# A rearranged prologue, transfers kept in written order, and loads spread over more slots in a Nystrom attention and feed-forward kernel

## The chip, the cores and the metric

The kernel runs on one core of one Trainium2 chip. The metric is the device time of one execution in microseconds (us). Three timed runs of the kernel before took 836.07, 836.29 and 840.3 us; their median is 836.29 us. One more execution was profiled, and it took 832.87 us.

## The reference

The attention runs over 4 batches, 8 heads, 576 positions and 64 features per head. It uses 32 landmarks, each the mean of 18 positions, and six Newton-Schulz steps for an inverse. Two feed-forward layers follow, both without biases:

```
q_lm, k_lm = means of 18 positions of q and k
A  = softmax(q @ k_lm^T / 8);  Bm = softmax(q_lm @ k_lm^T / 8);  C = softmax(q_lm @ k^T / 8)
Z  = Bm^T / (norm_1(Bm) * norm_inf(Bm) + 1e-6)
six times:  Z = 2 Z - Z @ Bm @ Z
x  = A @ Z @ C @ v                        # then heads side by side: 2304 tokens x 512
y  = ((x @ w_a) * (x @ w_b)) @ w_out      # 512 -> 1536 -> 512
h  = y @ w_in2
out = (h * tanh(softplus(h))) @ w_out2    # 512 -> 2048 -> 512
```

The three weights of the first layer and the two of the second lie in memory as 64-bit floats.

## The kernel before

**The work.** The whole program is one function, `nystrom_moe_kernel`. The attention of a batch is a list of steps: `kl`, `ql` (landmark sums), `sB` and `BB` (the landmark softmax and its norms), six `NS` (Newton-Schulz), `sC0`, `sC1` (scores of the landmarks against all keys), `ET0`, `ET1` (transposes), `U` (product with v), `M` (product of inverse and U, 128 x 128), `A0`, `A0n`, `A1`, `A1n` (scores of all queries, in two halves, and their normalisation). `fold` multiplies `M` into a block of the first layer's weights (tile `wab`) and gives `bm`, so that the first layer is `at` times `bm`. A slot (`ab`, then `emit_o1`) is 128 columns of the hidden layer for 288 tokens: 6 matmuls into bank `ps_ab` for each of w_a and w_b, their product `tg` on VectorE, its split in a high and a low part `g`, and 12 matmuls `ps_o<-g,wo` that add to the first output `x2acc`. There are 96 slots, and `CELLS` orders them by eights. Phase two takes 768 tokens at a time: seven products of 384 columns (`ps_ab<-xc,wc`) stand in for eight blocks, and `ps_o`, `ps_at` and `ps_bm` collect the output.

**Conversion.** Each 64-bit weight block of 128 x 512 (a unit) is loaded into a `stg` tile, turned to float32 by one ScalarE and four VectorE instructions (`to_f32`), and used or stored. The first layer has 36 units (24 for `wab`, 12 for `wo1`). The 32 of the second layer go through a buffer `f24` to memory (`wi2d`, `wo2d`) and are loaded again later.

**Order.** Up to slot 11 the order of TensorE, VectorE and ScalarE is written out by hand in the table `ORDER_1`, one word per piece: an attention step of batch 0, with `+` of batch 1, `cN` a piece of conversion unit N, `sN` of slot N, `oN` of an output, `f`/`F` a fold, and a bare number that many filling matmuls of the identity. `Written` holds instructions to program order while it is on. After slot 11 it is off: the loop over slots emits the work, and a scheduler that sees the whole program orders it. All transfers go out on one queue, SP, which issues them one by one; a transfer whose semaphore has not come holds those behind it.

**The places that the change touches.** In the prologue the landmark sums of batch 1 come from token tiles `tok` (`load_tokens`, L125; `lm_sum`, L162 on). They are 20 matmuls each for k and q: 128 tokens-by-feature columns are the fixed side, `blk` with 7 columns the moving one. `u0.prefetch` (L399) loads the units, eight of them early. In the slots, `load_wab` (L474) and `load_wo1` (L501) fetch weights again, `u2.step` runs the second layer's units from slot 45 to 84, `to_dram` (L604) stores each, and the store of `x2acc` (L586) follows its twelfth sum at once. `x_early` (from slot 82) prepares the first inputs of phase two, and its `weight_sums` puts two subtractions per weight on GpSimd (L430).

Of the kernel before, what the change touches and what calls it, by code (L numbers as in the profile page):

```python
# [31 lines left out]
def nystrom_moe_kernel(ctx: ExitStack, tc: tile.TileContext, q, k, v, w_a, w_b, w_out1, w_in2, w_out2, q1, k1, out):  # L32
# [35 lines left out]
    main = main_ctx.enter_context(tc.tile_pool(name="main", bufs=1, side="left"))  # L68
    p1_ctx = ExitStack()
# [16 lines left out]
    ist = const.tile([128, 1, 32], F32, name="ist")  # L86
    ist2 = ist.to_broadcast([128, 2, 32])
    blk = const.tile([128, 7], F32, name="blk")
# [3 lines left out]
    def consts():  # L92
        make_identity(nc, ident)
        gp.memset(bdm, 0.0)
        gp.memset(ones, 1.0)
        for h in range(4):
            gp.memset(bdm[32 * h:32 * h + 32, 32 * h:32 * h + 32], 1.0)
        ve.tensor_reduce(out=blk, in_=ident[:, 0:126].rearrange("p (l k) -> p l k", k=BLK), axis=AX, op=ALU.add)
        ve.tensor_reduce(out=ist[:, 0], in_=ident.rearrange("p (h l) -> p l h", h=4), axis=AX, op=ALU.add)
# [49 lines left out]
    def attention(ap, b, kt, qt, vt0=None, tokens=None):  # L149
# [226 lines left out]
    N_UNITS, N_SLOTS = 20, 12  # L376
    ORDER_1 = """
        kl kl ql ql c0 sB sC0 sB c0 sB sC1 4 c1 sC0 sB c2 sC1 BB 2 sC1 c3 BB sC1 sC1 c2 NS 2 c1 c3 NS ET0 NS
        c0 NS 2 c1 ET0 ET1 c3 c1 NS A0 ET1 NS c1 NS 1 A0 U NS A0 NS A0 c3 NS +kl U NS NS A0 c3 NS c0 +kl NS A0
        c0 NS +ql c2 c2 NS A0n c4 +ql NS +ql c5 c2 A0n M c6 +kl c5 M c5 A0n c5 f0 c7 A0n A1 c7 f0 c7 +kl A1 c8  # L380
        f0 +ql +kl A1 | s0 +ql c7 A1 +sC0 c5 +sC1 +sC0 s0 s0 A1 +sC1 s1 +sC1 A1 s0 c7 c6 s1 s1 A1n s0 s0 A1n
        c6 +sC1 s1 c6 +sC1 +sB c6 A1n +ET0 +sB s1 A1n +sB s1 +ET0 +sB s2 +ET1 c4 s2 c4 +BB c4 +ET1 s2 c4 +BB
        +U s2 c8 s2 +NS +U s2 s3 +NS +NS c8 +NS c8 s3 s3 +NS +NS c9 c8 +NS s3 f1 c8 c9 +NS +NS s3 c9 +NS c8 s3
        f1 c9 +NS c10 +NS f1 +NS +NS +NS s4 c10 c9 +NS s4 c10 s4 c9 +NS s5 s4 c10 s4 +M s5 s4 c10 s5 +M c9 c10
        s6 s5 c11 c10 +A0 s6 c11 s5 s6 c11 s5 c11 c12 s7 s6 c11 F0 s7 s6 +A0 c11 s6 s7 +A0 F0 +A1 c11 +A0 s7
        o0 F0 +A0 c12 o1 c12 +A0 c12 c12 o0 c13 F1 +A0n o1 s7 o2 c13 F1 s7 +A0n F1 +A0n o3 o2 +A0n c13 s8 c13
        c14 c13 o3 o4 s8 c14 c14 c14 c15 s8 +A1 o4 s9 c15 s8 o5 s9 +A1 s8 s8 c14 +A1 s9 c15 c15 c16 s10 s9 +A1
        c16 o6 c16 c16 s10 +A1 c15 s10 c16 o5 s11 +A1n o6 c17 o7 s9 s10 s11 +A1n s9 s10 c17 +A1n s11 s10 c17
        o7 c17 +A1n c18 s11 c18 s11 c18 s11 c17 c19 c18 c19 c19 c18 c19 c19
    """  # L390

    def stage(src, shape, early):

        tag, bufs = ("w", 8) if early else ("stg", 3)
        t = (main if early else base).tile([128, 512, 2], U32, tag=tag, bufs=bufs, name="stg")
# [36 lines left out]
    class Units:  # L432


        def __init__(self, units, early=0):
            self.units, self.st, self.n, self.ahead, self.early = units, [], 0, 2, early

        def prefetch(self, ahead=0):
            while len(self.st) < min(len(self.units), self.n + max(self.ahead, ahead)):
                src, shape, _ = self.units[len(self.st)]  # L440
                self.st.append(stage(src, shape, len(self.st) < self.early))
# [13 lines left out]
    def wab_units(g):  # L455
        def conv(i, jj, st):
# [3 lines left out]
            yield from to_f32(t[:, 2 * jj:2 * jj + 2, i], st, True)  # L460
            converted[g] = converted.get(g, 0) + 1
# [4 lines left out]
        for jj in range(2):  # L466
            for i, w in enumerate((w_a, w_b)):
                src = w.bitcast(U32)[256 * jj:256 * jj + 256, 512 * g:512 * g + 512].rearrange("(j p) f -> p j f", p=128)
                out.append((src, 2, lambda st, i=i, jj=jj: conv(i, jj, st)))
        return out  # L470

    def load_wab(g):
        t = wab[g] = main.tile([128, 4, 2, 256], F32, tag="wab", bufs=3, name="wab")
        nc.sync.dma_start(out=t.rearrange("p j i f -> p (j i f)"), in_=wabd[g])  # L474

    def split_unit(dst_hi, dst_lo, st):
# [9 lines left out]
        (gp if u0.n == 36 else ve).tensor_tensor(dst_lo, f3, dst_hi.bitcast(F32), op=ALU.subtract)  # L486

    wo1 = {}
    wo1d = [dram.tile([128, 2, DM], F32, name=f"wo1d{c}") for c in range(12)]

    def wo1_unit(c):
        def conv(st):
            wo1[c] = main.tile([128, 2, DM], F32R, tag="w", bufs=8, name="wo1")
# [5 lines left out]
    def load_wo1(c):  # L499
        wo1[c] = main.tile([128, 2, DM], F32R, tag="w", bufs=8, name="wo1")  # L500
        nc.sync.dma_start(out=wo1[c].bitcast(F32), in_=wo1d[c])  # L501
# [36 lines left out]
    def ab(b, g, hf, ch, gpool=None):  # L538
# [9 lines left out]
        if gpool is None:  # L548
            t = p1.tile([128, 2, 288], F32R, tag="g", bufs=9, name="g1")
# [10 lines left out]
    o1p, o1n = {}, {}  # L560

    def emit_o1(b, gp_, hf, d, part, now=True):
# [13 lines left out]
        def evict():  # L576
# [8 lines left out]
            if o1n[b, hf] == 12:  # L585
                nc.sync.dma_start(out=x2d[b][:, :, 288 * hf:288 * hf + 288], in_=x2acc[b, hf])  # L586
# [9 lines left out]
    f_pool = []  # L596

    def to_dram(dst, st):
        if f_pool:
# [472 lines left out]
```

## Time and profile before

| | |
|---|---|
| median of 3 timed runs | 836.29 us |
| profiled execution | 832.87 us |
| its span, first to last instruction | 830.8 us |
| mean granted TensorE clock | 0.982 |
| TensorE (PE) busy | 794.9 us, 96% |
| VectorE (DVE) busy | 545.8 us, 66% |
| ScalarE (ACT) busy | 359.3 us, 43% |
| GpSimd (POOL) busy | 144.1 us, 17% |
| moved by DMA | 183.45 MB, mean 221 GB/s |

PE, DVE, ACT and POOL are the four engines, PEld is TensorE loading its fixed side, and SP is the queue of transfers. A busy PE need not be at full speed, for a granted clock of 0.5 doubles the time of the same matmuls. A line number such as L56 belongs to a helper for most instructions, so groups are told apart by the tiles they write and read.

### The profile page before, as it was taken

To read this page: it belongs to the slowest core of one execution; us is meant where nothing else is said; L and a number is where in the kernel's file an instruction comes from. 1 tells how busy PE (TensorE), PEld (TensorE's weight loads), DVE (VectorE), ACT (ScalarE), POOL (GpSimd) and SP (SyncE) were. 2 spreads that over 40 slices of the span, in tenths; PEclk is the share of its full clock that TensorE was granted. 3 is DMA by queue.
4 is the path that set the end of the run, shared out by engine and by line. 5 is a ranking of instruction groups with operands and counts; after the bars stand their busy time and mean duration, and the time that the engine had idled before them with its cause. 6 is when DMAs were issued, how large, how long until landed. Compare 5 with 4: busy or idle time off the path is not lost.

```text
span 830.8 us, 14869 instructions
## 1 busy us (share of the span) xinstructions
PE 794.9 (96%) x5882; PEld 699.9 (84%) x5882; DVE 545.8 (66%) x1024; ACT 359.3 (43%) x826; POOL 144.1 (17%) x140
## 2 busy tenths in 40 slices
PE   5978899999999999899999999999999999999998
PEld 4766788987887797899899888998999999899997
DVE  7588897796585787988944767867433447433433
ACT  3555765434333544444533553454332335332332
POOL 0012022122240232222332354330000000000000
PEclk9679999999999999999999999999999999999999
DMA  9957567559326937978417887788654554654502
GB/s 333 341 207 242 191 231 242 187 166 332 128 87 217 361 99 258 330 247 308 130 58 269 295 298 258 291 302 332 239 213 182 190 188 179 251 212 171 190 1 76
DMA packets 48733, 183.45 MB, mean 221 GB/s; under 512 B 4260, under 2 KB 12452, under 8 KB 39320
## 3 DMA queue, kind: packets, MB, share of 16 engines
q1 hardware_dynamic: 48664, 182.51, 61.8%
q8 instruction: 46, 0.75, 0.4%
q14 instruction: 23, 0.19, 0.1%
HBM read 129.02 MB, written 53.48 MB: 220 GB/s over the span
## 4 chain that ended last, share of the span: by engine, by line
PE 76%; DVE 9%; DMA 7%; ACT 4%; issue 2%; POOL 1%; SPq 0%; DVEq 0%; ACTq 0%
PE ps_ab L56 33%; PE ps_o L56 23%; PE ps_bm L56 10%; PE ps_at L56 9%; DVE f L56 2%; DMA tok<-in_q_dram 2%; DMA s_out<-wo2d 2%; DMA wi2d<-f 2%; ACT sa L56 1%; DMA stg<-in_moe_w_a_dram 1%; DVE tg L56 1%; DMA stg<-in_moe_w_in_dram 1%; DVE f L413 1%; POOL wo L430 1%; DVE stA L56 1%
## 5 line engine op out<-in xcount | busy, mean ns | idle before, releaser
L56 PE MATMUL ps_ab<-xc,wc 128*128 128x384 f32 x1008 | 198.2, 336 | 1.8 <-DVE xc L56 1.1
L56 PE MATMUL ps_ab<-at,bm 128*128 128x288 f32 x1152 | 187.9, 304 | 3.8 <-DVE tg L56 2.8
L56 PEld LDWEIGHTS ps_ab<-xc,wc 128*128 128x128 f32 x1008 | 178.7, 188 | 13.1 <-DVE xc L56 1.4
L56 PE MATMUL ps_o<-g,wo 128*128 128x288 f32 x1152 | 180.0, 298 | 7.1 <-DVE x2acc L56 4.9
L56 PEld LDWEIGHTS ps_ab<-at,bm 128*128 128x128 f32 x1152 | 162.8, 191 | 25.6 <-issue 8.1
L56 PEld LDWEIGHTS ps_o<-g,wo 128*128 128x128 f32 x1152 | 161.0, 188 | 19.9 <-DVE x2acc L56 6.7
L555 POOL TENSOR_TENSOR g<-tg,g 128x288 fp32r<-128x288 f32 x96 | 84.8, 884 | 319.5 <-ACT g L56 319.5
L56 ACT ACTIVATE m<-c 128x384 f32<-128x384 f32 x95 | 49.7, 524 | 175.7 <-DVE c L56 175.3
L56 PE MATMUL ps_bm<-wo,g 128*128 128x512 f32 x288 | 93.4, 391 | 0.3 <-ACT g L56 0.3
L56 DVE TENSOR_TENSOR g<-m,g 128x384 fp32r<-128x384 f32 x96 | 66.0, 690 | 29.5 <-ACT g L56 29.4
L56 PE MATMUL ps_at<-wo,g 128*128 128x512 f32 x288 | 82.0, 391 | 0.0
L56 ACT ACTIVATE g<-tg 128x288 fp32r<-128x288 f32 x96 | 42.6, 444 | 86.3 <-DVE tg L56 85.9
L56 PE MATMUL ps_o<-wo,g 128*128 128x512 f32 x288 | 78.7, 391 | 0.9 <-DVE g L56 0.9
L56 DVE SCALAR_TENSOR_TENSOR f<-stg,f 128x512 uint32<-128x512 uint32 x88 | 68.8, 787 | 1.2
L56 DVE TENSOR_TENSOR tg<-ps_ab,ta 128x288 f32<-128x288 f32 x96 | 43.2, 451 | 31.3 <-PE ps_ab L56 17.1
L56 PEld LDWEIGHTS ps_at<-wo,g 128*128 128x128 f32 x288 | 53.9, 188 | 9.7
L56 PEld LDWEIGHTS ps_o<-wo,g 128*128 128x128 f32 x288 | 53.6, 188 | 10.1 <-DVE g L56 1.3
L56 PEld LDWEIGHTS ps_bm<-wo,g 128*128 128x128 f32 x288 | 53.3, 188 | 6.8 <-ACT g L56 0.6
L56 ACT ACTIVATE ta<-ps_ab 128x288 f32<-128x288 f32 x96 | 38.8, 405 | 42.8 <-PE ps_ab L56 42.2
L56 ACT ACTIVATE g<-m 128x384 fp32r<-128x384 f32 x96 | 50.2, 524 | 2.6
L56 DVE TENSOR_TENSOR c<-ps_ab,m 128x384 f32<-128x384 f32 x23 | 12.8, 558 | 48.2 <-PE ps_ab L56 48.2
L56 DVE TENSOR_TENSOR u2s<-ps_ab,m 128x384 f32<-128x384 f32 x24 | 13.3, 555 | 42.7 <-PE ps_ab L56 42.7
(150 smaller groups left out, 819.5 us busy)
## 6 DMA issues: line engine op xcount, KB each, us to landing
wc<-wcd SPq DMA_DIRECT2D x16, 1792.0 KB, 8.2
wo<-wod SPq DMA_DIRECT2D x16, 1024.0 KB, 5.5
stg<-in_moe_w_out_dram SPq DMA_DIRECT2D x28, 512.0 KB, 4.7
wcd<-wc SPq DMA_DIRECT2D x8, 1792.0 KB, 5.8
wab<-wabd SPq DMA_DIRECT2D x10, 1024.0 KB, 8.4
stg<-in_moe_w_in_dram SPq DMA_DIRECT2D x16, 512.0 KB, 5.8
wod<-wo SPq DMA_DIRECT2D x8, 1024.0 KB, 7.4
stg<-in_moe_w_a_dram SPq DMA_DIRECT2D x12, 512.0 KB, 3.6
```

Of the source, the lines that this page charges most:

```text
L56: i = f(*a, **kw)
L413: i = ve.engine.tensor_scalar(dst, dst, F32_TINY, F32_HUGE, op0=ALU.max, op1=ALU.min)
L430: lo_eng.tensor_tensor(dst_lo, src, dst_hi.bitcast(F32), op=ALU.subtract)
L555: gp.tensor_tensor(t[:, 1], tg, t[:, 0].bitcast(F32), op=ALU.subtract)
```

## The change

1. **Token sums.** The tokens are now the moving side: five matmuls of 32 x 512 per sum, four of them in different column groups, then a copy `lsum` on ScalarE and four matmuls of 128 x 32 with `sel` that gather and transpose.
2. **Prologue.** The first eight conversion units are joined in four of twice the width (`wab_units(..., double)`), so units 0 to 19 are now 0 to 15. The four later loads of them stand ahead of the token loads. `ORDER_1` is new: `sC0` and `sC1` come ahead of `sB`, and other fills stand between the `NS` steps.
3. **Written order.** `late` chains the transfers from slot 36 on, each issued after the one written before it.
4. **Stores later.** A store of `x2acc` is written four slots after its last sum, a store of a converted unit after the next unit's conversion.
5. **Loads spread.** Tables give the slot of each load (`WAB_AT`, `WO1_AT`, `X_AT`) and each unit (`U2_AT`, slots 38 to 80); from slot 56 unit loads run four ahead and use two more buffers.
6. **Around phase two.** The low parts in the early `weight_sums` go to VectorE in place of GpSimd; the first weight fetches and the splits for products 5, 4 and 3 are written among the last outputs of phase one, and all seven products of the first block are pinned.

```diff
@@ lm_sum (sums of tokens)
-                for j in range(4):
-                    for i in range(5):
-                        n, r = (4, 72) if i == 4 else (7, 126)
-                        f0 = DM * (i % 2) + 128 * j
-                        pe.matmul(p[:, LM * j + 7 * i:LM * j + 7 * i + n], ts[i // 2][0:r, f0:f0 + 128], blk[0:r, 0:n], start=True, stop=True)
-                    yield
+                for i in (1, 2, 3, 0, 4):
+                    r, g = (72, 0) if i == 4 else (126, i)
+                    pe.matmul(
+                        p[32 * g:32 * g + 32, :], blk[0:r, 0:32] if i == 4 else blk[0:r, 7:39], ts[i // 2][0:r, DM * (i % 2):DM * (i % 2) + DM],
+                        start=(i < 4), stop=(i > 0),
+                    )
+                yield
+                e = pg.tile([128, 2, 288], F32R, tag="g", bufs=4, name="lsum").bitcast(F32).rearrange("p a s -> p (a s)")
+                ac.activation(e[:, 0:DM], p, AF.Copy)
+                yield
+                p = bank("o1")
+                for j in range(4):
+                    pe.matmul(p[:, LM * j:LM * j + LM], e[:, 128 * j:128 * j + 128], sel, start=True, stop=True)
...
-    N_UNITS, N_SLOTS = 20, 12
+    N_UNITS, N_SLOTS = 16, 12
...
+    chain = []
+
+    def late(f):
+
+        def call(*a, **kw):
+            if not chain:
+                return f(*a, **kw)
+            if chain[-1] is None:
+                chain.append(f(*a, **kw).ins)
+                return
+            with tc.issue_after(chain[-1]):
+                chain.append(f(*a, **kw).ins)
...
@@ emit_o1, evict
             if o1n[b, hf] == 12:
-                nc.sync.dma_start(out=x2d[b][:, :, 288 * hf:288 * hf + 288], in_=x2acc[b, hf])
+                i = lambda: late(nc.sync.dma_start)(out=x2d[b][:, :, 288 * hf:288 * hf + 288], in_=x2acc[b, hf])
+                stores.append((at[0] + 4, i))
...
@@ to_dram
-        if f_pool:
-            f = f_pool[0].tile([128, 2 * 2 * TB], F32, tag="xe", bufs=4, name="f24")[:, 0:512]
+        n = u2.n - 1
+        if f_pool and n % 4 > 1:
+            f = f_pool[0].tile([128, 2 * 2 * TB], F32, tag="xf", bufs=2, name="f24")[:, 0:512]
...
-        nc.sync.dma_start(out=dst, in_=f if len(dst.shape) == 2 else f.rearrange("p (j f) -> p j f", j=dst.shape[1]))
+        while unit_stores:
+            unit_stores.pop()()
...
-    def weight_sums(dst, src, t):
+    def weight_sums(dst, src, t, lo=gp, pin=False):
...
@@ before the first table
-    u0.prefetch(4)
-    vt0 = load_v(ap, 0)
+    u0.prefetch(2)
+    vt0 = load_v(ap, 0)
+    u0.prefetch(4)
     tokens = load_tokens()
-    u0.prefetch(8)
...
-    LOAD_W = {5: 0, 6: 1, 7: 0, 8: 1, 9: 2}
-
+    X_AT = {78: -6, 80: -3, 81: -4, 82: 0, 83: 4, 84: -5, 86: 6, 88: 1, 89: 2, 90: 3, 92: 5}
+    U2_AT = [38 + 2 * n for n in range(6)] + [50 + 1.2 * n for n in range(26)]
+    WAB_AT = {37: 0, 38: 1, 42: 2, 49: 3, 52: 0, 56: 1, 62: 2, 66: 3, 72: 4, 75: 5}
+    WO1_AT = {40: 0, 41: 1, 43: 2, 44: 3, 50: 4, 51: 5, 52: 6, 53: 7, 76: 8, 77: 9, 78: 10, 79: 11}
...
-        if ci in LOAD_W and ks in (2, 5):
-            load_wab(2 * LOAD_W[ci] + ks // 4)
-        if ci in (5, 6, 9) and ks >= 4:
-            load_wo1(4 * LOAD_W[ci] + ks - 4)
+        if si in WAB_AT:
+            load_wab(WAB_AT[si])
+        if si in WO1_AT:
+            load_wo1(WO1_AT[si])
```

**TensorE, prologue, batch 0 from the fifth Newton-Schulz step to the first slot.** In these rows `rz` is a Newton-Schulz step, `zd,U` is `M`, `wab,mt` a fold, `qt,kl` is `A1`, and `at,bm` a slot. Before, around `M`:

```order
L56 MATMUL ps_o_490<-blk,tok 128x4
L56 MATMUL ps_o_490<-blk,tok 128x7 x4
L56 MATMUL ps_o_490<-blk,tok 128x4
L56 MATMUL ps_at<-zd,U 64x128 x2
L56 MATMUL ps_o_444<-blk,tok 128x7 x4
L56 MATMUL ps_o_444<-blk,tok 128x4
L56 MATMUL ps_bm<-wab,mt 32x512 x8
L56 MATMUL ps_at<-qt,kl 32x288 x8
L56 MATMUL ps_o_444<-blk,tok 128x7 x4
```

Now:

```order
L56 MATMUL ps_at<-rz 32x64 x8
L56 MATMUL ps_o_472<-ident 128x128 x2
L56 MATMUL ps_at<-rz 32x32 x8
L56 MATMUL ps_o_496<-ident 128x128
L56 MATMUL ps_at<-zd,U 64x128 x2
L56 MATMUL ps_o_510<-tok,blk 32x512 x5
L56 MATMUL ps_at<-qt,kl 32x288 x8
L56 MATMUL ps_bm<-wab,mt 32x512 x8
L56 MATMUL ps_o_551<-tok,blk 32x512 x5
L56 MATMUL ps_o_567<-sel,lsum 128x32 x4
L56 MATMUL ps_ab<-at,bm 128x288 x6
```

All 40 token matmuls stood ahead of the first slot, 25 of them ahead of `M`; now no token matmul stands ahead of `M`, and ten wide ones and four of 128 x 32 stand ahead of the first slot.

**VectorE, prologue, from the start values of Newton-Schulz (`rz<-bc,stB`).** `wab` is conversion. Before:

```order
L56 TENSOR_TENSOR rz<-bc,stB 128x64
L413 TENSOR_SCALAR wab<-wab 128x2x256 x3
L56 TENSOR_TENSOR rz<-ps_at,rz 128x64
L56 TENSOR_SCALAR wab<-wab 128x2x256 x3
L56 SCALAR_TENSOR_TENSOR wab<-stg,wab 128x2x256
L56 TENSOR_TENSOR rz<-ps_at,rz 128x64
```

Now, from a little earlier:

```order
L56 STREAM_TRANSPOSE bc<-bc 128x32 x2
L56 TENSOR_SCALAR wab<-wab 128x1024
L452 TENSOR_SCALAR wab<-wab 128x1024
L56 TENSOR_REDUCE stB<-ps_at 128x2x2
...
L56 TENSOR_TENSOR rz<-bc,stB 128x64
L56 SCALAR_TENSOR_TENSOR wab<-stg_168,wab 128x1024
L56 TENSOR_TENSOR rz<-ps_at,rz 128x64
L56 TENSOR_SCALAR wab<-wab 128x1024
```

Three wide conversion instructions now stand ahead of the start values, where one narrow one stood, and one wide one between one step and the next. At the reduction for batch 1's `sC0` 23 of the 32 narrow instructions of the first eight units were done; now 15 of the 16 wide ones are.

**SP, around the second loads of the first layer's saved weights.** `wabd` holds these weights, `stg` is a 64-bit load, `f` a converted unit. Before:

```order
L474 DMA wab<-wabd_84 128x2048
L604 DMA wi2d_102<-f_3288 128x512
L399 DMA stg<-in_moe_w_out_dram 128x1024
L474 DMA wab<-wabd_85 128x2048
L604 DMA wi2d_102<-f_3355 128x512
L399 DMA stg<-in_moe_w_in_dram 128x2x512
```

Now:

```order
L418 DMA x2d_84<-x2acc 512x1x288
L438 DMA stg<-in_moe_w_in_dram 128x2x512
L438 DMA stg<-in_moe_w_out_dram 128x1024 x2
L418 DMA wo2d_115<-f_3881 128x512
L418 DMA wab<-wabd_88 128x2048
L438 DMA stg<-in_moe_w_in_dram 128x2x512
L418 DMA wo2d_115<-f_3956 128x512
```

Two loads of `wab`, a megabyte each, stood one unit apart; now one stands here, with a store of `x2acc` between, and each store of a unit stands behind the load of a later unit.

## Rows read from the trace of the kernel before

**Rows 1.** Page: granted TensorE clock in 40 slices, in tenths.

```profile
PEclk9679999999999999999999999999999999999999
```

**Rows 2.** Stretches: span, busy time per engine, granted clock, DMA share, GB/s.

```profile
25.30:49.20 23.90, 23.53 (x178) 19.16 (x177) 13.17 (x28) 11.49 (x49) 0.00 (x0) 0.50 0.98 360
49.20:112.00 62.80, 53.41 (x595) 42.95 (x587) 55.47 (x124) 42.82 (x156) 9.74 (x11) 0.95 0.58 202
112.00:190.00 78.00, 77.98 (x602) 67.42 (x602) 66.26 (x127) 36.42 (x79) 18.48 (x20) 1.00 0.61 206
190.00:250.00 60.00, 58.24 (x646) 49.63 (x645) 39.15 (x81) 22.15 (x51) 17.89 (x20) 1.00 0.49 173
250.00:345.00 95.00, 90.89 (x925) 75.55 (x924) 73.76 (x152) 42.96 (x93) 22.74 (x25) 1.00 0.71 255
400.00:443.00 43.00, 39.88 (x293) 38.82 (x292) 28.40 (x51) 20.38 (x40) 18.36 (x17) 1.00 0.33 116
443.00:490.00 47.00, 44.30 (x240) 40.21 (x240) 29.92 (x44) 20.32 (x36) 15.89 (x9) 1.00 0.86 298
490.00:827.00 337.00, 336.69 (x1688) 303.71 (x1686) 174.24 (x292) 125.90 (x232) 26.78 (x12) 1.00 0.56 206
```

**Rows 3.** TensorE in order of time, prologue: start, length, instructions, wait before.

```profile
16.42 0.43 PE L56 MATMUL ps_at<-rz 32*32 32x64 f32 x16 [1.39 <-DVE rz L56]
22.96 0.61 PE L56 MATMUL ps_o<-blk,tok 126*128 126x7 f32 x4
...
29.55 1.44 PE L56 MATMUL ps_o<-blk,tok 126*128 126x7 f32 x6 [0.37 <-DMA tok<-in_q_dram]
30.92 0.44 PE L56 MATMUL ps_at<-rz 32*32 32x32 f32 x16
31.29 4.43 PE L56 MATMUL ps_o<-blk,tok 126*128 126x7 f32 x20
35.65 0.70 PE L56 MATMUL ps_at<-zd,U 128*64 128x128 f32 x4
...
38.50 1.96 PE L56 MATMUL ps_bm<-wab,mt 64*32 64x512 f32 x16
...
45.63 1.79 PE L56 MATMUL ps_ab<-at,bm 128*128 128x288 f32 x6
47.35 1.21 PE L56 MATMUL ps_at<-kt,ql 64*32 64x288 f32 x16
...
66.07 0.43 PE L56 MATMUL ps_at<-rz 32*32 32x64 f32 x16
...
67.42 0.43 PE L56 MATMUL ps_at<-rz 32*32 32x64 f32 x16
67.78 1.09 PE L56 MATMUL ps_bm<-wab,mt 64*32 64x512 f32 x16
```

**Rows 4.** VectorE in order of time, prologue.

```profile
26.56 0.42 DVE L56 TENSOR_SCALAR wab<-wab 128x512 uint32<-128x512 uint32 x1
44.27 1.28 DVE L56 SCALAR_TENSOR_TENSOR wab<-stg,wab 128x512 uint32<-128x512 uint32 x2
48.67 0.76 DVE L56 TENSOR_REDUCE stC<-ps_at 128x2 f32<-128x576 f32 x1 [3.12 <-PE ps_at L56]
...
111.92 0.45 DVE L56 TENSOR_TENSOR tg<-ps_ab,ta 128x288 f32<-128x288 f32 x1
```

**Rows 5.** Waits of TensorE: total us, times, longest.

```profile
PE ps_o L56 <- DVE x2acc L56: 4.9, 4, 1.9
```

**Rows 6.** SP in order of time: the load of batch 1's keys.

```profile
31.58 0.33 SPq L111 DMA_DIRECT2D kt<-in_k_dram  x1
```

**Rows 7.** DMA issues: KB each, median us from issue to landing.

```profile
kt<-in_k_dram SPq DMA_DIRECT2D x3, 1152.0 KB, 13.3
```

**Rows 8.** Chain of work that ended last, 240 to 345 us: start, length, what.

```profile
267.95 9.66 DMA wi2d<-f
...
325.85 5.77 DMA stg<-in_moe_w_in_dram
```

More of the change, by code (lines that the diff above doesn't have):

```diff
@@ new lines, in stage @@
+    def stage(src, shape, early, spare=None):
+        if early:
+            t = main.tile([128, 2 * DM, 2], U32, tag="w", bufs=4, name="stg2")
+            v = t.rearrange("p (j i f) w -> p j i (f w)", j=2, i=2)
+            for i, a in enumerate(src):
+                late(nc.sync.dma_start)(out=v[:, :, i], in_=a)
+            return t
+        if spare:
+            t = spare.tile([128, 2 * 7 * 2 * 128], F32, tag="we", bufs=2, name="stg")
+            t = t[:, 0:1024].bitcast(U32).rearrange("p (n w) -> p n w", w=2)
+        else:
+            t = base.tile([128, 512, 2], U32, tag="stg", bufs=3, name="stg")
@@ L459, in conv @@
             t = wab[g]
-            yield from to_f32(t[:, 2 * jj:2 * jj + 2, i], st, True)
-            converted[g] = converted.get(g, 0) + 1
+            half = t[:, 2 * jj:2 * jj + 2]
+            yield from to_f32(half.rearrange("p j i f -> p (j i f)") if double else half[:, :, i], st, True)
+            converted[g] = converted.get(g, 0) + 1 + double
             if converted[g] == 4:
@@ L499, in load_wo1 @@
     def load_wo1(c):
-        wo1[c] = main.tile([128, 2, DM], F32R, tag="w", bufs=8, name="wo1")
-        nc.sync.dma_start(out=wo1[c].bitcast(F32), in_=wo1d[c])
+        wo1_tile(c)
+        late(nc.sync.dma_start)(out=wo1[c].bitcast(F32), in_=wo1d[c])
     bm = {}
@@ L641, in load_quad @@
             n = min(TB - off, S - s0)
-            nc.sync.dma_start(out=t[:, :, off:off + n], in_=x2d[b][:, 2 * half:2 * half + 2, s0:s0 + n])
+            late(nc.sync.dma_start)(out=t[:, :, off:off + n], in_=x2d[b][:, 2 * half:2 * half + 2, s0:s0 + n])
             off += n
@@ L678, in x_early @@
                     load_quad(t[:, h], *f)
-            for w in range(2 if n == 0 else 0):
+        elif n == -4:
+            for w in range(2):
                 early["w", w] = stg([128, 4, 256], "s_in")
-                nc.sync.dma_start(out=early["w", w], in_=wi2d[w])
+                late(nc.sync.dma_start)(out=early["w", w], in_=wi2d[w])
         elif n == 1:
@@ L881, in nystrom_moe_kernel @@
     u2s = plus(early_product(6), m1, "u2s")
+    split_x(0, 5, early["t1"])
     last_o1()
-    c11 = plus(early_product(2), m1, "c11")
+    p = early_product(2)
+    ve.tensor_tensor(m1, p[:, 0:TB], m1, op=ALU.add)
+    split_x(0, 4, early["t4"])
     last_o1()
-    u3s = plus(early_product(7), u2s, "u3s")
+    split_x(0, 3, early["22"])
     last_o1()
     last_o1()
-    p1_ctx.close()
-    px = ctx.enter_context(tc.tile_pool(name="px", bufs=1, side="right", reuse_waits="tile"))
+    pg_ctx.close()
+    for _, store in stores:
+        store()
     main_ctx.close()
@@ L996, in nystrom_moe_kernel @@
         for gap, k in enumerate(ORDER):
-            p = None if n == 0 and k in ORDER[:4] else product(k, n)
+            if gap == 1 and n in (1, 2):
+                last_stores.pop(0)[1]()
+            if n == 0:
+                p = None if k in ORDER[:3] else early_product(k)
+            else:
+                p = product(k, n)
             if p is None:
-                if k == 2:
-                    mish(0, 0, c11)
+                pass
             elif k == 1:
```

177 lines of the change are left out of this document (104 added, 73 removed).

## The prediction

> **What bounds the kernel now.** I read the granted clock first, then the engines by stretch, then the prologue in order of time, then the waits and the chain. The clock [rows 1] shows slow slices only near the start. By stretches [rows 2] phase two, 490 to 827 us, has TensorE busy for 336.69 of 337 us: nothing is to be had there without less work, and the change takes no work out of it. From 112 to 190 us TensorE is busy for 77.98 of 78 us, while VectorE has 11.7 us left. What TensorE loses lies in three places:
>
> - At 25.3 to 49.2 us it is busy for 23.53 of 23.9 us, but the granted clock is 0.50, its 1.2 GHz level [rows 2].
> - At 49.2 to 112 us it idles for 9.4 of 62.8 us. VectorE is busy for 55.47 us, 88% [rows 2]: with waits of chains between engines in it, this stretch is as good as bound by VectorE.
> - Later it idles for 1.8 us (190 to 250), 4.1 us (250 to 345), 3.1 us (400 to 443) and 2.7 us (443 to 490), together 11.7 us [rows 2].
>
> In the first place the reader is to see what stands in line. Batch 0's last Newton-Schulz step runs at 30.92 us, behind token sums that waited for their DMA; `M` follows at 35.65 us behind 4.43 us of token sums; the fold stands at 38.50 us, and the first slot at 45.63 us [rows 3].
>
> **The change, part by part.** The sum is made against the profiled execution's own 832.87 us, which lies 3.4 us under the median of 836.29 us.
>
> *Token sums.* Twenty matmul records of 7 columns take 4.43 us at half clock [rows 3]; 40 matmuls are 80 records, so some 17.7 us at that clock and 9 at the full one. The new form has no row. The nearest is the fold, 16 records of 512 columns in several column groups: 1.09 us at full clock, 1.96 at half [rows 3]. A sum is one such pass over four groups and a fifth matmul after it, so I take two passes: 2.2 or 3.9 us. The four gathering matmuls are near four token records, 0.61 us [rows 3], or 1.2 at half clock. Two sums then cost 5.6 us at full and 10.2 at half clock. The gain is some 3 to 12 us of TensorE time, all before the first slot.
>
> TensorE's clock fell at 25.3 us, in the midst of 7-column matmuls, with the engine nearly always busy [rows 2, 3]. The Trainium skill's page "TensorE: Matmul & The Clock Gate", part 1, says that the clock follows how busy the engine has been. By that alone this stretch would have stayed at full speed, and wide tokens would return nothing through the clock; the row speaks against it. The sum here does not use the clock beyond the two prices above.
>
> *Chain to the first slot.* Newton-Schulz starts at 16.42 us [rows 3]. Ahead of it VectorE now has three wide conversion instructions, where one narrow one stood. A narrow one takes 0.42 us [rows 4] and a wide one, by its elements, 0.84, so the start slips by 2.1 us to 18.5. Two unhindered steps stand 1.35 us apart (66.07 and 67.42) [rows 3]. Between them VectorE now has wide instructions of 0.84 or 1.28 us (two narrow ones in a row took 1.28 [rows 4]), so a step takes 1.4 to 2.0 us; I take 1.8. Five steps more end the chain at 27.5 us in place of 30.92, and `M`, 4.73 us after the last step before, can come about 1.5 us after it, at 29 us. Then stand a sum, `A1`, the fold and the other sum. At full clock the fold ends at 33, at half at 37; from fold to first slot 7.1 us passed before, of which 4.43 were tokens, and the rest, 2.7, stays. The first slot would come at 36 to 41 us in place of 45.63: 5 to 9 us earlier.
>
> *What is late next.* The loads between: SP puts four conversion loads ahead of the tokens, 2.1 MB, which at the 360 GB/s of this stretch [rows 2] is 6 us; the last tokens, waited for at 29.55 us [rows 3], land at up to 35.5 us. That is behind the fold, and mostly covered by it. Batch 1's keys are the firmer floor. Their load was issued at 31.58 us [rows 6], and loads of this kind took 13.3 us to land [rows 7], so about 45 us; the DMA share is 0.98 there [rows 2], and the bytes ahead of it stay the same. Its first use was at 47.35 us [rows 3], so batch 1 starts only some 2.5 us earlier, 5 if its load fares better. The remaining earliness of batch 0 turns into slots done while batch 1 waits.
>
> *VectorE after that.* From batch 1's `sC0` (48.67 us) to the twelfth product `tg` (111.92 us) [rows 4] VectorE is the limit. By the order of the program this piece loses 12 narrow conversion instructions of its 32 for `wab` (six of each kind, less one wide): 6 x 0.42 + 6 x 0.64 - 1.28 = 5.1 us. Some other 3 us (one `bm`, one `at`, one normalisation) move ahead of it or behind it. Those moved behind lie under a stretch where TensorE is full and VectorE has 11.7 us free [rows 2]; without that cover they cost their 2 us again. Of the 8 us I count three quarters, since chains of batch 1 (steps 1.35 us apart) also hold. The twelfth product is then earlier by 2.5 + 6 = 8.5 us. Bounds: 3, if only the keys' earliness comes through, and 15, if batch 0's whole 9 us and 6 more do.
>
> *Second layer's units, stores and loads.* On the chain a store of a converted unit took 9.66 us to land, and a load 5.77 us [rows 8]. The first waits for its buffer, one of two; VectorE, kept in order, waits with ScalarE behind it, and `tg` behind those. Spreading loads and running four ahead should take most of the 4.1 us at 250 to 345. I take 2.5. At 400 to 443 TensorE waits for `x2acc` on VectorE, 4.9 us in all over the kernel [rows 5]. Units now end at slot 80 and not 84, but 3.8 us of subtractions come from GpSimd (1536 elements per weight, 0.64 us per 512 [rows 4], two weights). I take 1 of the 3.1 us. At 443 to 490 the splits and fetches are written earlier: 1.5 of 2.7 us. The 1.8 us at 190 to 250 precedes the chained transfers and stays. Together 5 us, bounds 0 and 9.
>
> *At nothing.* A store four slots later lies under slots: 96 of them from 45.63 us [rows 3] to about 443 us [rows 2] are 4.1 us each, four 16.6; if a buffer of `x2acc` is wanted sooner, the next sum waits for the landing. Fills stand where TensorE waits anyway.
>
> The sum: 832.87 - 8.5 - 5 = 819.4 us, and with the 3.4 us that the median stands above it, **822.8 us**. A difference under 0.5%, 4.2 us, can't be told from no change.
>
> **The rivals.**
>
> *A. The clock and the keys eat the prologue.* Between the later steps there now stand one or two fills and no token sums. If the clock falls there already, the sums cost 10.2 us, and the first slot comes at 41 or 42; with keys at 45 us only 3.5 us remain. For it: rows at 0.50 with TensorE nearly full. Against it: the wide tokens and the fold follow at once, and the clock came back at 49.2 us [rows 2] while the fold and the first slots ran. 836.3 - 3.5 - 5 = 827.8 us. The page named above would have a thinly used engine fall to the lower level, which speaks for this one, as far as steps with few fills are thin use; the trace has no such stretch.
>
> *B. The later waits only move.* A store now waits for the next unit, and until slot 56 there are still two buffers. At 1.2 slots per unit, 4.8 us, a buffer is wanted again after 9.6 us, but store and landing (4.8 + up to 9.66 [rows 8]) can take 14.5. Then the prologue alone counts: 836.3 - 8.5 = 827.8 us. For it: the 9.66 us row; against it: that row is the longest, and the loads that crowded it are spread.
>
> *C. Slower: the fixed order blocks SP.* A load of `wab` or `wo1` waits for TensorE to free its buffer, and now everything written later stands behind it, unit loads above all. The chain has 10 and 12 of these. If each holds a unit back by 0.8 us that reaches TensorE, the 17.6 us outdo 8.5 and the result is 845 us. It decides from 0.4 us per load on, where the prologue is used up. Against it: unit loads run four ahead, some 19 us, and by the tables a buffer's last fold lies before its next load in each case.
>
> *D. The change takes more.* Batch 0's whole earliness comes through (12 us) and 8 of the 11.7 us later: 816 us.
>
> *E. It doesn't do what it says.* The prologue's order is one of many waits, and VectorE's 88% was the bound all along, with the deferred work paid later; nothing else moves: 834 us.
>
> **How the numbers follow.** The forecast, prologue and part of the later waits, 0.5; A 0.14; B 0.14; D 0.11; E 0.06; C 0.05. Likeliest is 822.8 us. Leaving out most of C and E and a tail beyond D, the range is 810 to 832.5 us; its lower end is 836.3 - 15 - 9 = 812 with 2 us for the median's scatter, its upper end the low bounds 3 and 0 with half a microsecond. Faster by over 0.5% holds for the forecast, A, B and D, less an edge of A and B: 0.86. Within: E and that edge, 0.09. Slower: C, 0.05.
>
> **What would show it.** Right: the first slot near 38 us, batch 1's `sC0` near 44, the twelfth product near 103; a granted clock of 0.5 for less than 24 us; idle time of TensorE at the second layer's units under 2 us. Wrong: the first slot early but the twelfth product after 108 (the VectorE step), SP waits at `wab` loads with unit loads late behind them (C), or ScalarE waiting for a store of `f` at slots 50 to 56 (B).

## The result and the profile after

The changed kernel took 842.77 us (median of 11 runs, 840.95 to 845.66), the kernel before in the same set 838.89 us (836.07 to 841.05). The ratio is 1.0057, 95% interval 1.0039 to 1.0076: slower by 4.8 us by this ratio, where 13.5 us less were forecast. (The ratio is an estimate from all executions of both kernels and not the quotient of the two medians, which stand 3.9 us apart.) The profiled execution took 842.19 us with a span of 840.4; that of before, 832.87 us, was a quick one, for in all later sets its kernel had medians of 836 to 836.5. The two profiles therefore stand 9.3 us apart, about twice what the medians and the ratio show.

The same stretches of the changed kernel, columns as in [rows 2], and the clock of its page, to be held against [rows 1]:

```profile
25.30:49.20 23.90, 18.95 (x191) 9.38 (x189) 17.88 (x35) 16.52 (x85) 0.00 (x0) 0.76 1.00 327
49.20:112.00 62.80, 54.33 (x600) 43.71 (x601) 55.08 (x117) 41.19 (x142) 11.71 (x12) 0.96 0.59 206
112.00:190.00 78.00, 76.88 (x648) 67.18 (x647) 65.47 (x124) 37.43 (x80) 18.70 (x21) 1.00 0.62 215
190.00:250.00 60.00, 58.10 (x595) 49.56 (x588) 43.17 (x90) 22.04 (x49) 16.80 (x18) 0.97 0.59 205
250.00:345.00 95.00, 90.76 (x891) 75.57 (x890) 68.97 (x149) 41.35 (x92) 23.64 (x25) 0.98 0.61 210
400.00:443.00 43.00, 40.31 (x308) 38.76 (x307) 27.23 (x47) 17.93 (x36) 10.63 (x12) 1.00 0.35 110
443.00:490.00 47.00, 45.05 (x258) 42.11 (x257) 26.27 (x43) 19.34 (x34) 12.02 (x8) 0.96 0.48 172
490.00:827.00 337.00, 335.93 (x1686) 303.21 (x1685) 167.12 (x291) 125.86 (x232) 31.81 (x15) 1.00 0.59 222
```

```profile
PEclk9879999999999999999999999999999999999999
```

The first row is what the new prologue was to do: TensorE is busy for 18.95 us in place of 23.53 and its clock is 0.76 in place of 0.50. At 250 to 345 us nothing is won: it still idles for 4.2 us, and at a clock of 0.98. A fixed window of time says little about a program that has shifted, so the products `tg` were counted instead, one per slot, by their starts on VectorE:

| product | before | changed | difference |
|---|---|---|---|
| 1st | 50.6 | 50.9 | +0.3 |
| 12th | 111.9 | 105.0 | -6.9 |
| 13th | 115.2 | 113.2 | -2.0 |
| 33rd | 190.8 | 188.3 | -2.5 |
| 45th | 243.3 | 243.1 | -0.2 |
| 61st | 315.3 | 321.6 | +6.3 |
| 85th | 405.5 | 417.6 | +12.1 |
| 93rd | 435.0 | 443.1 | +8.1 |

The changed kernel is ahead by 2.5 us at the 33rd product. The 2.3 us lost from there to the 45th are lost without the chain of transfers too (2.2 us in the profile of that run, below). The great loss comes between the 45th and the 85th, where the transfers are chained.

The 12th product is 6.9 us early and the 13th only 2.0. The stretches from batch 1's first reduction (`stC`) to the 12th product and from there to the 13th, before:

```profile
48.67:111.92 63.25, 53.86 (x603) 42.95 (x587) 55.92 (x123) 43.35 (x160) 9.74 (x11) 0.94 0.58 201
111.92:115.25 3.33, 3.31 (x24) 3.09 (x23) 3.30 (x7) 1.61 (x4) 0.91 (x1) 1.00 0.00 0
```

and in the changed kernel:

```profile
48.24:105.01 56.77, 49.84 (x577) 38.65 (x562) 49.67 (x107) 37.67 (x135) 10.90 (x11) 0.94 0.62 214
105.01:113.18 8.17, 6.63 (x50) 6.40 (x50) 6.17 (x11) 4.11 (x9) 0.81 (x1) 1.00 0.43 159
```

Up to the 12th product VectorE has 6.3 us less to do, and the stretch is 6.5 us shorter. But much of this work now stands behind the 12th product: 6.17 us of VectorE's work lie before the 13th, where 3.30 lay.

TensorE in order of time in the prologue of the changed kernel, to be held against [rows 3]:

```profile
30.09 0.33 PE L56 MATMUL ps_at<-rz 32*32 32x32 f32 x16 [0.87 <-DVE rz L56]
...
31.31 0.80 PE L56 MATMUL ps_at<-zd,U 128*64 128x128 f32 x4 [0.47 <-DVE zd L56]
32.04 3.64 PE L56 MATMUL ps_o<-tok,blk 126*32 126x512 f32 x10
...
38.02 1.93 PE L56 MATMUL ps_o<-tok,blk 126*32 126x512 f32 x10
39.88 1.08 PE L56 MATMUL ps_o<-sel,lsum 128*128 128x32 f32 x8
40.79 1.10 PE L56 MATMUL ps_ab<-at,bm 128*128 128x288 f32 x6
43.42 1.10 PE L56 MATMUL ps_o<-sel,lsum 128*128 128x32 f32 x8 [1.53 <-ACT lsum L56]
...
46.94 1.22 PE L56 MATMUL ps_at<-kt,ql 64*32 64x288 f32 x16 [0.81 <-DMA kt<-in_k_dram]
```

`M` comes at 31.31 us in place of 35.65, the first slot at 40.79 in place of 45.63. But batch 1's first scores start at 46.94 us, where they started at 47.35, and they wait for the keys.

Now the place where time was lost. SP in order of time at 246 to 270 us, in the changed kernel:

```profile
246.38 1.01 SPq L418 DMA_DIRECT2D wo2d<-f  x1
247.44 0.53 SPq L418 DMA_DIRECT2D x2d<-x2acc  x1
256.71 0.33 SPq L143 DMA_DIRECT2D vt<-in_v_dram  x1
268.36 0.33 SPq L438 DMA_DIRECT2D stg<-in_moe_w_out_dram  x1
268.74 0.43 SPq L418 DMA_DIRECT2D wi2d<-f  x1
269.27 0.38 SPq L418 DMA_DIRECT2D wab<-wabd  x1
```

what VectorE does for the unit that is stored at 268.74 us (the last of its conversion):

```profile
266.88 1.42 DVE L56 SCALAR_TENSOR_TENSOR f<-stg,f 128x512 uint32<-128x512 uint32 x2
```

and what TensorE does there, with the whole program's waits for `wab` and `x2acc`, again of the changed kernel:

```profile
262.20 1.09 PE L56 MATMUL ps_bm<-wab,mt 64*32 64x512 f32 x16
...
269.88 1.09 PE L56 MATMUL ps_bm<-wab,mt 64*32 64x512 f32 x16
...
276.69 1.95 PE L56 MATMUL ps_bm<-wab,mt 64*32 64x512 f32 x12 [2.79 <-DMA wab<-wabd]
```

```profile
PE ps_o L56 <- DVE x2acc L56: 3.4, 3, 1.6
PE ps_o L56 <- ACT x2acc L56: 3.3, 2, 1.7
PE ps_bm L56 <- DMA wab<-wabd: 3.1, 2, 2.8
```

Between 247.97 and 268.36 us SP issues one transfer. Then, at once, a unit's load, a unit's store, and the load of `wab` that the fold at 276.69 us waits for. The store could not go before VectorE had converted the unit, at 268.30 us, and the `wab` load was written after the store. The buffer of the load was free earlier: without the chain (below) the same load goes out at 262.39 us, 0.1 us behind a fold, and that fold ends here at 263.29. So a load whose buffer had been free for some 6 us stood behind a store whose data did not exist yet. Twelve matmuls of the fold then take 1.95 us where sixteen had taken 1.09 at 269.88 us: the wait also cost the clock, which was granted at 0.50, the lower level, just after it:

```profile
276.69:278.60 1.91, 1.91 (x13) 0.25 (x13) 0.00 (x0) 0.00 (x0) 0.00 (x0) 0.50 1.03 395
```

The Trainium skill's page "TensorE: Matmul & The Clock Gate", part 1, says that the clock follows how busy the engine has been; the trace agrees here, with 2.79 us of waiting and 0.50 behind it.

Further on the chain of work that ended last, 300 to 335 us, runs through such stores:

```profile
302.91 7.94 DMA wo2d<-f
...
316.67 5.11 DMA wi2d<-f
...
326.03 6.96 DMA wo2d<-f
```

Each is issued within half a microsecond of the load of a later unit (302.50, 316.24 and 325.60 us in the same view), which SP had waited to place, and ScalarE waits for each landing before it can use the buffer `f` again.

### The profile page after: what moved, and what is told of

Its sections match the earlier page's. It is cut to its first block, busy times and chain, and to the rows that moved or that the text cites. A ratio compares the mean times of both kernels' runs of the same rounds, so it can differ in the third digit from the quotient of the medians.

```text
span 840.4 us, 14779 instructions
## 1 busy us (share of the span) xinstructions
PE 797.9 (95%) x5854; PEld 693.3 (82%) x5854; DVE 537.6 (64%) x1012; ACT 360.6 (43%) x824; POOL 140.9 (17%) x143
## 4 chain that ended last, share of the span: by engine, by line
PE 71%; DMA 11%; DVE 10%; ACT 4%; issue 3%; SPq 1%; DVEq 0%; ACTq 0%
PE ps_ab L56 31%; PE ps_o L56 19%; PE ps_bm L56 11%; PE ps_at L56 9%; DMA kt<-in_k_dram 3%; DMA wo2d<-f 2%; DVE f L56 2%; DMA wi2d<-f 1%; DMA xq<-x2d 1%; ACT sa L56 1%; DMA stg<-in_moe_w_a_dram 1%; DMA stg<-in_moe_w_out_dram 1%; DMA wab<-wabd 1%; DVE wab L56 1%; DVE xt L56 1%
## 5 line engine op out<-in xcount | busy, mean ns | idle before, releaser
L605 POOL TENSOR_TENSOR g<-tg,g 128x288 fp32r<-128x288 f32 x96 | 88.3, 920 | 340.0 <-ACT g L56 278.1
L56 DVE TENSOR_TENSOR g<-m,g 128x384 fp32r<-128x384 f32 x96 | 60.1, 627 | 29.0 <-ACT g L56 28.5
```

Of the source, the lines that this page charges most:

```text
L56: i = f(*a, **kw)
L605: gp.tensor_tensor(t[:, 1], tg, t[:, 0].bitcast(F32), op=ALU.subtract)
```

## The experiments

All ratios are to the kernel before, run beside them on the same chip. They lie up to 2.5 us off the quotients of the medians, so smaller differences between runs of different sets aren't read. Two theories: **the chain** of transfers costs what the change brings (rival C, with another mechanism); or **the stores written later** and the new tables do (rival B). Beside it stood the question why the prologue brought 2.5 us and not 8.5.

**Without the chain.** `late` returns the plain call; everything else stays.

```diff
-            if not chain:
-                return f(*a, **kw)
+            if True:
+                return f(*a, **kw)
```

> The changed kernel without the chain: transfers from slot 36 on are ordered by the scheduler again; tables, deferred stores and prologue stay. Theory (the fixed order makes everything written later stand behind a load that waits for its buffer, and slots 44 to 84 lost 10.5 us by it): the time falls by 7 to 11 us from 842.8, to 832 to 836, and the product tg of slot 84 comes some 10 us earlier. Rival (the deferred stores hold the two buffers of the converted units, or the tables fetch too late, with or without the chain): 841 to 845 us.

Measured: 832.29 us, ratio 0.9941 (0.9920 to 0.9963), against 1.0057 with the chain. SP in the same place, without the chain:

```profile
261.17 0.80 SPq L413 DMA_DIRECT2D wo<-wo1d  x2
262.39 0.32 SPq L413 DMA_DIRECT2D wab<-wabd  x1
263.73 0.79 SPq L413 DMA_DIRECT2D wo<-wo1d  x2
265.07 0.52 SPq L413 DMA_DIRECT2D x2d<-x2acc  x1
265.92 0.83 SPq L413 DMA_DIRECT2D wab<-wabd  x1
267.36 0.33 SPq L438 DMA_DIRECT2D stg<-in_moe_w_out_dram  x1
267.74 0.43 SPq L413 DMA_DIRECT2D wi2d<-f  x1
```

Two loads of `wab` are now out before the unit's store; the wait for `wab` is gone from the list of TensorE's waits. The unit itself is converted no sooner (store at 267.74 us, against 268.74). The 85th product starts at 412.2 us, 5.4 us earlier than in the changed kernel (10 were expected), the 93rd at 437.1, 6.0 us earlier, and the span ends 8.8 us earlier (831.6 us): the last 2.8 us of this come after the 93rd.

**The chain alone.** The kernel before, with nothing but `late` around the same stores and loads.

```diff
-        nc.sync.dma_start(out=t.rearrange("p j i f -> p (j i f)"), in_=wabd[g])
+        late(nc.sync.dma_start)(out=t.rearrange("p j i f -> p (j i f)"), in_=wabd[g])
...
+        if si == 36:
+            chain.append(None)
```

> The kernel before with the chain alone: its own prologue, tables, stores at once; every store and load that the change chains is chained from slot 36 on. Theory (a fixed written order makes loads of wab and wo1 stand behind stores that wait for VectorE, whatever the tables): 6 to 12 us slower than before, ratio 1.007 to 1.014. Rival (the chain only hurts with the deferred stores and the new tables): 0.999 to 1.003.

Measured: 846.37 us, ratio 1.0116 (1.0082 to 1.0149): 9.7 us slower, as much as taking it from the changed kernel gave back (1.0057 less 0.9941 is 0.0116). So the chain needs neither the tables nor the stores written later to cost this. TensorE's waits for `wab` in this run, where the list of the kernel before has none:

```profile
PE ps_bm L56 <- DMA wab<-wabd: 4.7, 3, 3.4
```

**Stores at once, chain kept.**

```diff
-                stores.append((at[0] + 4, i))
+                i()
...
-        unit_stores.append(lambda: late(nc.sync.dma_start)(...))
+        late(nc.sync.dma_start)(...)
```

> The changed kernel with the chain, but a store of x2acc and of a converted unit is written at once and not four slots or one unit later. Theory (loads that wait for their buffers block the chained order): no gain, 841 to 846 us, or slower, since a store at once stands ahead of fetches while its data is still being made. Rival (the deferral keeps each of the two buffers of converted units for one unit more, and the units wait for it): 835 to 838 us.

Measured: 841.81 us, ratio 1.0071 (1.0048 to 1.0095), no better than the changed kernel. Writing the stores later is not what costs; rival B falls.

**Which transfers of the chain.** One run takes the loads of `wab` and `wo1` out of the chain, another the stores of converted units, a third starts the chain only at phase two.

```diff
@@ loads of wab and wo1 out of the chain
-        late(nc.sync.dma_start)(out=t.rearrange("p j i f -> p (j i f)"), in_=wabd[g])
+        nc.sync.dma_start(out=t.rearrange("p j i f -> p (j i f)"), in_=wabd[g])
@@ unit stores out of the chain
-        unit_stores.append(lambda: late(nc.sync.dma_start)(out=dst, ...))
+        unit_stores.append(lambda: nc.sync.dma_start(out=dst, ...))
@@ chain from phase two
-        if si == 36:
-            chain.append(None)
```

> The changed kernel with the chain, but the loads of wab and wo1 are not part of it; stores and fetches of phase two still are. Theory (the loads of wab and wo1 stood behind stores and unit loads that waited for VectorE, and TensorE waited 3.1 us for wab, with a lower clock after it): wab arrives in time, and 4 to 8 us come back, 835 to 839 us. Rival (what costs is that the unit stores, one behind the other, hold ScalarE and VectorE at slots 52 to 84): under 2 us come back, 841 to 843.

> The changed kernel with the stores of converted units taken out of the chain; loads of wab and wo1, stores of x2acc and fetches stay in it. Theory (a load of wab or wo1 stands behind a store that waits for VectorE's conversion): 6 to 9 us come back, as without the loads in the chain, 0.995 to 0.999 of before. Rival (the loads are also held behind x2acc's stores and each other's buffers): under 3 us come back, 1.002 or more.

> The changed kernel with the chain only from the first product of phase two on; the slots 36 to 95 are left to the scheduler. Theory (the chain costs in the slots): as the run without the chain, 0.992 to 0.996 of the kernel before. Rival (part of the cost is at the start of phase two, where fetches wait for stores): 2 us or more over that, 0.997 to 1.000.

Measured: 0.9974 (0.9948 to 1.0000), 0.9971 (0.9951 to 0.9991) and 0.9935 (0.9908 to 0.9962). Against 1.0057 the first two give back 6.9 and 7.2 us of the 9.7; it doesn't matter which of the pair leaves the order, the load or the store. Phase two's own chain costs nothing that can be measured. So most of the price is one pair: a load with a free buffer behind a store with no data. The last 2.5 us are less than these intervals can place. TensorE's own waits for `wab` are only 3.1 us in the changed kernel; by which waits the rest of the price reaches the end was not followed one by one.

**The new prologue alone, and the rest alone.** The first run is the kernel before with the new token sums, double units, table and pool of the prologue. The second is the reverse: all later parts of the change, no chain, and the prologue of before.

```diff
@@ the kernel before with the new prologue
-    N_UNITS, N_SLOTS = 20, 12
+    N_UNITS, N_SLOTS = 16, 12
...
@@ the changed kernel with the prologue of before, no chain
-    N_UNITS, N_SLOTS = 16, 12
+    N_UNITS, N_SLOTS = 20, 12
...
+    def late(f):
+        return f
```

> The kernel before with the new prologue alone (tokens as the moving side, double units, its table, its pool), all later transfers and tables as before. Theory (the traces show the prologue ahead by 2.5 us at slot 32, and the loss comes only after slot 36): 2 to 3.5 us under the kernel before, ratio 0.996 to 0.998. Rival one (my prediction of the prologue: 8.5 us, hidden in the changed kernel by something else): ratio 0.990. Rival two (the earliness is given back later in any case, since the later stretch is set by transfers): ratio 0.999 to 1.002.

> The prologue of before (its token sums, units, table) with all the rest of the change except the chain: spread loads, deferred stores, the start of phase two. With the new prologue this was 0.9941 of the kernel before; the new prologue alone was 1.0055. Theory one (the new prologue brings its 2.5 to 3 us, and in the kernel before it only met the start of phase two badly): 2 to 3.5 us over the run without the chain, ratio 0.997 to 0.999. Theory two (the new prologue costs in itself, in both): ratio 0.985 to 0.990, faster than every other run.

Measured: 1.0055 (1.0033 to 1.0077), outside all three expectations, and 0.9947 (0.9922 to 0.9972), below theory one and above theory two. With the new later parts the new prologue is worth 0.5 us (0.9941 against 0.9947), which is nothing that can be told; with the old later parts it costs 4.6. In the profile of the first run the products are ahead by 2.8 us at the 45th, behind by 1.6 at the 57th, ahead by 0.3 at the 61st and behind by 2.5 at the 96th; 5.9 us more are lost behind the 96th, in phase two (the span is 839.2 us against 830.8). What stands between the 45th and the 57th, in the chain of that run and among its waits at 240 to 300 us:

```profile
266.01 11.18 DMA wi2d<-f
```

```profile
ACT f L429 <- DMA wi2d<-f: 5.7, 1, 5.7
```

It is the store of [rows 8], which took 9.66 us: the first of a unit, issued among the loads of `wab` (1024 KB) and `wo1` (512 KB). ScalarE waits 5.7 us for it. It can be a part of the loss at most, since the greater part lies behind the 96th product.

**Prologue and unit times as a square.** The new times of the second layer's units (first at slot 38) were put into the kernel before, with the new prologue and without it. A third run puts the old times into the fastest version (no chain, keys first; below), with the last store of a unit at slot 85.

```diff
-        if si == 44:
+        if si == 36:
...
-        if si > 44:
-            u2.step(min(32, 32 * (si - 44) // 40) - u2.n)
+        while si > 36 and u2.n < 32 and si >= U2_AT[u2.n]:
+            u2.step()
@@ the third run
-    U2_AT = [38 + 2 * n for n in range(6)] + [50 + 1.2 * n for n in range(26)]
+    U2_AT = [44 + 1.25 * (n + 1) for n in range(32)]
```

> The kernel before with the new prologue and the new times of the second layer's units (first at slot 38, last at 81); no chain, stores at once, other tables as before. Theory (the earliness of the prologue was lost to units crowded into slots 45 to 60, and moving units alone cost 6 us in the fastest version): ratio to before 0.992 to 0.997, 5 us or more under the prologue alone (1.0055). Rival (it was lost at the start of phase two, where this kernel is as before): 1.001 to 1.006.

> The kernel before with the new times of the second layer's units alone. Theory (spreading helps by itself): ratio 0.992 to 0.997. Rival (the whole later part brought only 2.75 us with the old prologue, so the units' times bring less there): 0.998 to 1.002.

> The fastest version so far (830.95 us) with the second layer's units at the slots of the kernel before (every 1.25 slots up to 84, none before slot 46), and the last store of one at slot 85. Theory (six units done before slot 50 and an end at slot 80 take the load off slots 56 to 84): 3 to 5 us slower, 834 to 836 us, slots 76 to 84 later. Rival (the spreading does nothing once the transfers are free): 830 to 832 us.

| ratio to before | units as before | units spread |
|---|---|---|
| prologue of before | 1 | 1.0014 (0.9992 to 1.0037) |
| new prologue | 1.0055 (1.0033 to 1.0077) | 0.9985 (0.9964 to 1.0007) |

The third run: 837.21 us, 1.0007 (0.9985 to 1.0029), where the fastest version is at 0.9905. So the spreading gives 5.9 us (1.0055 less 0.9985) and 8.5 us (1.0007 less 0.9905; 6.3 by the medians) with the new prologue and nothing with the old one. Against what was expected, 0.9985 lies between theory and rival, 1.0014 is the rival's, and 837.21 us is above both. In both kernels with the new prologue and the old times the first units' store is on the chain (11.18 us above, 11.71 in the third run); with the new times six units are gone before slot 50 and no such store is. With the new prologue and the new times in the kernel before, 2.3 us are lost behind the 96th product in place of 5.9. That the store is the cause is not shown: the old prologue gets by with the old times, at 9.66 us for the same store, and the runs don't settle why.

**Keys first, with and without the chain.** The three loads of w_out blocks are issued after the first load of batch 1's keys.

```diff
-    run1 = attention(ap, 1, *load_qk(ap, 1), None, tokens)
-    u0.prefetch(7)
+    keys = []
+    run1 = attention(ap, 1, *load_qk(ap, 1, keys), None, tokens)
+    with tc.issue_after(keys[0]):
+        u0.prefetch(5)
...
```

> The changed kernel with three prologue loads of w_out blocks issued after the first load of batch 1's keys and not before it. Theory (the landing of batch 1's keys is the floor of the prologue): the keys land 4 to 5 us earlier, sC of batch 1 starts at 42 to 43.5 us in place of 46.94, the tg of slots 4 to 32 come 2 to 4 us earlier, and the time falls by as much if nothing later takes it, to 839 to 841. Rival (VectorE, 88% busy behind it, is the bound from the first product on): sC earlier, tg from slot 12 on unchanged within 1 us, 842 to 843.5 us.

> The changed kernel without the chain and with three w_out loads issued behind the first load of batch 1's keys. In the profile of the run with keys first and the chain, slots 4 to 36 stood 1.2 to 2 us ahead of the changed kernel, and the chain took it away later. Theory (without the chain an earliness of the prologue reaches the end): 1 to 2.5 us under the run without the chain, ratio to the kernel before 0.991 to 0.993. Rival (the stretch from slot 44 on is set by the transfers, whatever came before it): as the run without the chain, 0.994, or over it.

Measured: with the chain 841.61 us, 1.0058 (1.0037 to 1.0080); without it 830.95 us, 0.9905 (0.9875 to 0.9936). The keys' load moved from 31.87 to 25.44 us, and the scores of batch 1 from 46.94 to 43.66, in the profile with the chain:

```profile
25.44 0.36 SPq L119 DMA_DIRECT2D kt<-in_k_dram  x1
```

```profile
43.66 0.72 PE L56 MATMUL ps_at<-kt,ql 64*32 64x288 f32 x16 [0.84 <-DMA kt<-in_k_dram]
```

The keys were the floor, as supposed. Of the 3.3 us, 2.0 are there at the 33rd product, and with the chain nothing reaches the end: 841.61 us lies between the two expectations. Without the chain the kernel is 7.9 us under the kernel before by the ratio, 5.5 by the medians, and it serves as the fastest version below. Its interval overlaps that of the run without the chain alone, so a gain from the keys (3 us by the ratios, 1.3 by the medians) isn't shown.

**Less work for VectorE.** In that fastest version the last two of the five conversion instructions are left out for units 4 to 11.

```diff
+        if merge:
             ve.scalar_tensor_tensor(du, hi, 0xC0000000, du, op0=ALU.bitwise_and, op1=ALU.bitwise_or)
         yield
+        if merge:
             ve.scalar_tensor_tensor(du, lo, 29, du, op0=ALU.logical_shift_right, op1=ALU.bitwise_or)
```

> The fastest version so far (no chain, keys first; 830.95 us) with sixteen VectorE instructions left out between the first slot and the twelfth product: the last two of the conversion of eight blocks (units 4 to 11), so signs and low bits of these weights are left out. They take about 0.65 us each, 10 us in all. Theory (my step: from batch 1's sC to the twelfth product VectorE is the limit, so work taken from it moves the product by three quarters): tg of slot 12 comes 6 to 9 us earlier, and the time is 5 us or more lower, 823 to 826. Rival (chains between engines hold there, ScalarE and the evictions of x2acc among them; VectorE merely looks full): tg of slot 12 under 2.5 us earlier, 829 to 831 us.

Measured: 829.15 us, 0.9904 (0.9867 to 0.9942), in total as with these instructions. The 13th product starts at 107.9 us, against 110.3 in the fastest version. By itself this says little, since the same prologue had it at 108.2 and 113.1 us in two other profiles. But that scatter lies ahead of the 5th product. From the 5th to the 13th product the twelve other profiles of the new prologue take 41.1 to 42.0 us, and this one takes 37.6. The stretch in the fastest version and then in this one:

```profile
68.50:110.34 41.84, 37.36 (x304) 31.62 (x298) 36.52 (x70) 30.93 (x115) 7.94 (x8) 0.96 0.54 185
```

```profile
70.25:107.86 37.61, 35.98 (x317) 30.51 (x316) 29.78 (x59) 29.45 (x114) 8.15 (x9) 1.00 0.56 187
```

VectorE has 6.7 us less to do there, and the stretch is 3.5 to 4.4 us shorter. So VectorE's work counts in this stretch, by half to two thirds of what was taken out, and the theory is right so far; but the time follows the rival. The lead on the fastest version is 2.5 us at the 33rd product, 1.0 at the 93rd and 0.9 at the end of the span; on the profile of the next run it is 5.1, 1.3 and 0.7. A lead of the prologue is lost between the 33rd and the 93rd product, and which wait takes it was not found.

**Low parts on GpSimd again**, in the fastest version.

```diff
-            weight_sums(t, early["w", w], stg([128, 4, 2, 128], "s4"), ve)
+            weight_sums(t, early["w", w], stg([128, 4, 2, 128], "s4"))
```

> The fastest version so far (830.95 us) with the low parts of the early weight sums back on GpSimd, as in the kernel before. Theory (VectorE had room there and GpSimd was late at the start of phase two): 1 to 2.5 us slower, 832 to 833.5 us. Rival (work off the path that decides): 830 to 831.5 us.

Measured: 830.9 us, 0.9929 (0.9900 to 0.9958). The rival holds: this part of the change does nothing that can be measured.

## Why the prediction was wrong

- **Rival C was dismissed by the wrong buffers.** This step failed. It asked whether a `wab` load finds its buffer freed by TensorE ("by the tables a buffer's last fold lies before its next load in each case"), and at the load looked at above that was so. It feared for the unit loads that stand behind; but `late` doesn't chain these, and the loads of `wab` and `wo1` are what came late. It didn't ask what else stands in one written order: stores, which wait for VectorE to make their data. The blocked transfers were the loads of `wab` themselves, and what blocked them were unit stores: taking either out of the chain gave back some 7 of the 9.7 us that the chain costs. Size and chained loads were in the text (22 loads, deciding from 0.4 us per load on; the 9.7 us measured are 0.44 per load), with a chance of 0.05; the sum itself had no term for the chain. The order rows ahead of the prediction show a `wab` load right behind a store of `f`; the conversion's place on VectorE was not looked up beside it.
- **The VectorE step counted at a mark that work was moved past.** This step failed too. Up to the 12th product it came out: 6 us were forecast from batch 1's `sC0` on, and the stretch is 6.5 us shorter with 6.3 us less work for VectorE. The product came at 105.0 us, under the 108 named as a sign against the step. But the work that was moved behind the mark was put at some 2 us and lying under cover, while 6.17 us in place of 3.30 now stand before the 13th product, TensorE idles for 1.5 of the 8.17 us there, and the 13th is 2.0 us early. The run with less work for VectorE bears out that its work counts there, and that a lead won there is not kept.
- **The chain to the first slot was right, at the edge of its range.** 40.79 us, in the range of 36 to 41; `M` came at 31.31 us where 29 was reckoned. The token sums took 1.93 and 3.64 us (2.2 and 3.9 expected) and the clock was at its lower level for less than before.
- **The keys were the floor, at 46.94 us and not at 45.** Their load went out at 31.87 us and the scores waited for it until 46.94, 15.1 us, where 13.3 was the median of [rows 7]. So 0.4 us came through in place of 2.5.
- **The later waits came near in size, if the chain is set aside, and this may be luck.** 5 us were forecast; all later parts without the chain, on the old prologue, gave 4.4 (0.9947; 2.8 by the medians). Of their parts the low parts gave nothing, and the unit times nothing alone. Most of the forecast was to be won in the slots, but in the profile of that run the 93rd product is 1.7 us later than in the one of before, and 2.3 us are won behind it. So the waits that were named are not shown to have given it.
- **What the prologue earned didn't add up with the rest.** The sum took its 8.5 us as kept to the end. In the profiles with the prologue as in the changed kernel 2.5 to 5.2 us reach the 33rd product; the ratios give 0.5 us with the new later parts and -4.6 with the old.

Without the chain the forecast of 13.5 us would still have missed: 4.9 us were there (0.9941).

## What to carry to other kernels

A fixed order on one queue of transfers is safe only if every transfer in it is ready no later than the next one is needed: list the stores too, look up when their data is made, and keep loads with free buffers out from behind them. A mark in the program, such as the twelfth product, shows a gain that isn't one when work has been moved behind it: count at a later mark too. An engine's work can hold a stretch, and taking it away still bring nothing at the end; leave some of it out and see how far the lead gets before counting on it. Gains ahead of a crowded stretch of transfers don't add to the changes in that stretch, so each pair wants a square of runs.

## What the hardware showed that was not expected

The same prologue, with the same instructions, had a granted clock between 0.75 and 0.90 from one execution to the next. Two rows of 17 to 70 us, of the run with low parts on GpSimd and of the one with the old unit times, which don't differ before slot 36:

```profile
17.00:70.00 53.00, 45.96 (x653) 29.00 (x644) 40.73 (x97) 30.64 (x120) 2.92 (x3) 0.75 0.89 299
```

```profile
17.00:70.00 53.00, 43.75 (x667) 28.35 (x665) 45.40 (x107) 32.69 (x126) 4.53 (x5) 0.90 0.90 313
```

Their 13th products start at 113.1 and 108.2 us. So the start of a product in a single profile of this prologue is uncertain by some 5 us, more than what the whole new prologue was worth; the stretch from the 5th product to the 13th is not, at 41.1 and 41.8 us in these two.
